# A fused attention and two-layer kernel on one core: new order of the first three attention groups, identity products on TensorE, and a new order of the exponential in the middle stage

## The chip, the cores and the metric

The kernel runs on one core of a Trainium2 chip. A core has TensorE (PE; its weight loads are shown apart, as PEld), VectorE (DVE), ScalarE (ACT), GpSimd (POOL) and SyncE (SP), which here issues nearly all DMAs. Each engine takes its instructions in the order in which the program issues them to it. The metric is the time of one execution in microseconds (us) on the device.

## The reference

Chunked attention (batch 4, 8 heads, 768 tokens, 64 wide; chunks of 32 queries look at 16 keys before the chunk, the chunk, 8 keys after it, and 8 memory keys) is followed by two dense blocks over 3072 tokens:

```python
x = attention(q, k, v, mem_k, mem_v)          # 3072 x 512
h = x @ w_in                                  # 512 -> 2048
x = where(h > 0, h, exp(min(h, 0)) - 1) @ w_out   # 2048 -> 512
out = ((x @ w1) * (x @ w2)) @ w3 @ w_out2     # 512 -> 1024 -> 1024 -> 512
```

All inputs and outputs are fp32.

## The kernel before

**Precision.** Each fp32 operand of the large products is split into a high part (a cast on ACT, `hi`) and a rest (a subtraction on DVE, `lo`), and each product becomes three (`mm3`, L124 to L126). The weights come raw from memory (512 KB a job); the `Feed` prepares a job in three `feed.step()` calls: `rebase` on ACT, `shift` and `low` on DVE a step later, then `hi_of` on ACT and `lo_of` on DVE (L172, L175) another step later. A step also issues the load of a job four to eight places on. There are 32 such jobs.

**Attention** works on 24 groups of 128 queries. A group passes through ten stages: `at_turn` (eight transposes on PE, three copies on ACT), `at_turn2`, `at_scores` (64 small products), `at_max` (DVE, then the exponential on ACT), `at_sum`, `at_norm`, `at_flip` (DVE), `at_values` (64 small products), `at_out` (hi on ACT, lo on DVE). `load_qk` and `load_v` issue its DMAs on SP in pieces of 256 bytes a row and head. Groups 1 and 2 have tiles of their own; group 3 and all later ones use the tiles of group 0.

**Start.** The first three groups fill the 384 tokens of block 0. The order of their stages and of the first five feed steps (`f`) is written out by hand in the string `START` (L69): `t u s m z n p v o` with a digit are the stages of that group. After it come the loads of group 3 (L607, L608). The feed's first five raw loads and all loads of groups 0 to 2 are issued ahead of it.

**Main loop.** Step n (0 to 129) belongs to block j = n // 16 and feature tile f = n % 16. It has `mm_h(n)` (12 matmuls into the PSUM bank `PS[4 + n % 2]`), `elu_exp(n)` (two ACT operations that read that bank), `elu_max(n)` (DVE, last reader of the bank, so `mm_h(n + 2)` waits for it), `elu_hi` (ACT), `elu_lo` (DVE), and `mm_x(n - 2)` (12 matmuls). In the first two steps of a block `mm_x(n - 2)` comes ahead of `mm_h(n)`, elsewhere behind it. In step 16j + 1 `store_x1` copies the finished block out of PSUM: four copies, alternately on ACT and DVE, through the pool `f_p` of four buffers, which the jobs of the middle stage use too, and four DMAs to `x1d`. While n < 16 there are two feed steps in each step.

**Slots.** `at_step()` is called twice in a step and works off one slot each time. Group G's stages start at slot `base(G)` and lie at +0 (turn), +1 (turn2, load of the next group's q and k), +2 (scores), +3, +4, +5, +6 (flip), +8 (values, out), +9 (load of the next group's v). From group 6 on, each group brings one to three conversion jobs of later weights (rebase at +0, low at +1, split at +2, store to memory in the next slot; a second kind at +4, +5 and +9, with four transposes on PE, `mid_flip`).

After step 129 the weights of the second dense block are multiplied together, and the rest is dense products. The change touches none of that.

Of the kernel before, what the change touches and what calls it, by code (L numbers as in the profile page):

```python
# [19 lines left out]
def tile_kernel(  # L20
# [24 lines left out]
    P = 128  # L45
# [15 lines left out]
    GPB = TB // GQ  # L61
    FF1 = w_in.shape[1] // P
# [3 lines left out]

    LATER = (10, 11, 12, 13, 14, 15, 25, 26, 27, 28, 29, 30, 31)

    START = "t0 u0 f s0 t1 f m0 u1 s1 z0 n0 m1 p0 t2 v0 u2 s2 f z1 n1 p1 o0 m2 v1 f z2 n2 p2 o1 v2 f o2"  # L69
    SCALE = 1.0 / float(D) ** 0.5  # L70
    assert GQ == P and KEYS == 64 and KT == 4 and HP == 4 and DM == 512

# [8 lines left out]
    ident = const.tile([P, P], F32, name="ident")  # L81
# [168 lines left out]
    def load_qk(G):  # L250
        if G >= NG:
            return
        b, g = divmod(G, GPS)
        t0 = g * GQ - LEFT
        p0, n1 = max(0, -t0), min(LEFT + RIGHT, S - t0 - P)
        kn_g = k_t[G] = at_tile(G, qk_p, [P, 2, H, D], "kn") if 0 < G < GPB else kn
        q_t[G] = at_tile(G, qk_p, [GQ, H, D], "qn")
        eng = nc.scalar if G == 0 else nc.sync
        eng.dma_start(out=q_t[G], in_=by_token(q, b, g * GQ, (g + 1) * GQ))
        nc.sync.dma_start(out=kn_g[p0:P, 0], in_=by_token(k, b, t0 + p0, t0 + P))  # L260
        nc.sync.dma_start(out=kn_g[0:n1, 1], in_=by_token(k, b, t0 + P, t0 + P + n1))
        if g == 0 or G < GPB:
            nc.sync.dma_start(out=kn_g[LEFT + RIGHT:CH, 1], in_=by_token(mem_k, b, 0, NM))

    def load_v(G):
        if G >= NG:
            return
        b, g = divmod(G, GPS)
        t0 = g * GQ - LEFT
        p0 = max(0, -t0)  # L270
        vw_g = v_t[G] = at_tile(G, v_p, [P, 2, H, D], "vw") if 0 < G < GPB else vw
        nc.sync.dma_start(out=vw_g[p0:P, 0], in_=by_token(v, b, t0 + p0, t0 + P))
        for c in range(NCG):
            t1 = t0 + (c + 1) * CH
            n1 = min(LEFT + RIGHT, S - t1)
            nc.sync.dma_start(out=vw_g[c * CH:c * CH + n1, 1], in_=by_token(v, b, t1, t1 + n1))
            if g == 0 or G < GPB:
                nc.sync.dma_start(out=vw_g[c * CH + LEFT + RIGHT:(c + 1) * CH, 1], in_=by_token(mem_v, b, 0, NM))
# [147 lines left out]
        slots.setdefault(int(at), []).append((at, len(slots.get(int(at), ())), fn, arg))  # L426

    def base(G):
        return 2 * FF1 * (G - GPB) // GPB, "slow"

    GM = 2 * GPB
    others = [Job((raw_rows, w_out2, c, 0), store=wod[c]) for c in range(FF2)]
# [21 lines left out]
    def at_step():  # L454
        store_next()
        for _, _, fn, arg in sorted(slots.pop(slot_at[0], ()), key=lambda x: x[:2]):
            fn(arg)
        slot_at[0] += 1
# [19 lines left out]
    def elu_max(n):  # L478
        e = eg_t[n]
        nc.vector.scalar_tensor_tensor(out=e, in0=e, scalar=-1.0, in1=h_t.pop(n), op0=ALU.add, op1=ALU.max)  # L480
# [5 lines left out]
    def elu_lo(n):  # L486
        g = g_t[n]
        nc.vector.tensor_tensor(out=g[:, 1, :], in0=eg_t.pop(n), in1=g[:, 0, :].bitcast(F32), op=ALU.subtract)  # L488
# [82 lines left out]
    with tc.manual_schedule():  # L571
        def weight(i):
            if i < FF1:
                return Job((raw_cols, w_in, i), slot=i)
            return Job((raw_rows, w_out, i - FF1, 0), slot=i)

        jobs, due = [], {}
        order = sorted(range(2 * FF1), key=lambda i: i if i < FF1 else i - FF1 + 2)
        for i in order:
            due[i] = len(jobs)  # L580
            jobs.append(weight(i))
        first_late = min(due[i] for i in LATER)
        feed = Feed(jobs)

        load_qk(0)
        make_identity(nc, ident)
        nc.gpsimd.memset(kn[0:LEFT, 0], 0.0)
        nc.gpsimd.memset(vw[0:LEFT, 0], 0.0)
        for c in range(NCG):
            for s in range(2):  # L590
                nc.gpsimd.memset(odd[c * CH:(c + 1) * CH, s], float(c % 2 == s))
        feed.load(1)
        load_qk(1)
        feed.load(2)
        load_v(0)
        load_qk(2)
        load_v(1)
        feed.load(3)
        load_v(2)
        feed.load(5)  # L600
        one = dict(t=at_turn, u=at_turn2, s=at_scores, m=at_max, z=at_sum, n=at_norm, p=at_flip, v=at_values, o=at_out)
        for what in START.split():
            if what == "f":
                feed.step()
            else:
                one[what[0]](int(what[1]))
        load_qk(GPB)  # L607
        load_v(GPB)  # L608
        early_psum.close()
        psum_x = ctx.enter_context(tc.tile_pool(name="psum_x", bufs=1, space=PSUM))  # L610
        for i in range(KT):
            PS[i] = psum_x.tile([P, 512], F32, name=f"bank{i}")
        NH = NB * FF1
        for n in range(NH + 2):
            j, f, at, last = seq[n] if n < NH else (NB, n - NH, n - NH, False)
            first = at < 2 and n >= 2
            if j == NB - 1 and f == 0:
                store_next()
                mid_ctx.close()
                at_ctx.close()  # L620
                late = ctx.enter_context(tc.tile_pool(name="late", bufs=1, side="right"))
                ab_jobs = [(c, r) for c in range(FF2) for r in range(2)]
            if n == FF1:
                feed.until(len(feed.jobs) - 1)
                raw_ctx.close()
                mid_ctx = ExitStack()
                pools["raw"] = mid_ctx.enter_context(tc.tile_pool(name="raw2", bufs=2, side="right"))
                pools["st"] = mid_ctx.enter_context(tc.tile_pool(name="st_p", bufs=2, side="right"))
                mid_load(2)

            def x():
                if n >= 2:
                    if n < FF1 + 2:
                        feed.until(due[FF1 + seq[n - 2][1]])
                    mm_x(n - 2)
                    if at == 1 and n < NH:
                        store_x1(j - 1)
                if n < FF1:
                    feed.step()
                at_step()  # L640

            if first:
                x()
            if n < NH:
                if j == 0:
                    feed.until(due[f])
                mm_h(n)
            if 1 <= n <= NH:
                elu_hi(n - 1)
            if n < FF1:  # L650
                feed.step()
            if 1 <= n <= NH:
                elu_lo(n - 1)
            at_step()
            if n < NH:
                elu_exp(n)
            if not first:
                x()
            if n < NH:
                elu_max(n)  # L660
            if n >= NH - FF1:

                free = [f] if n < NH else []
                if n >= NH - FF1 + 2:
                    free.append(FF1 + n - 2 - (NH - FF1))
                for slot in free:
                    if len(s_wo) < FF2 and len(s_wo) <= len(s_w3):
                        fill(slot, wod[len(s_wo)])
                        s_wo.append(slot)
                    elif len(s_w3) < 2 * FF2:  # L670
                        half, c = divmod(len(s_w3), FF2)
                        fill(slot, w3d[half][c])
                        s_w3[half, c] = slot
                    else:
                        c, r = ab_jobs.pop(0)
                        fill(slot, wabd[c][r])
                        s_ab[c, r] = slot
            if j == NB - 1:
                if f == 4:
                    load_x1(0)  # L680
                if f == 8:
                    split_x1(0)
                    load_x1(1)
        store_x1(NB - 1)
        for half in range(2):
            for c in range(FF2):
                for i in range(KT):
                    mm_wc(half, c, i)
                    if c == FF2 - 1:
                        keep_wc(half, i)  # L690
            for i in range(KT, FF2):
                c, r = ab_jobs.pop(0)
                fill(s_w3[half, i], wabd[c][r])
                s_ab[c, r] = s_w3[half, i]
        NA = NB * FF2
        for n in range(NA + 1):
            j, f = divmod(n, FF2)
            if n < NA:
                mm_ab(n)
                if f == 2 and j + 1 < NB:  # L700
                    split_x1(j + 1)
                    if j + 2 < NB:
                        load_x1(j + 2)
            if n >= 1:
                mm_o(n - 1)
                if f == 0:
                    store_out(j - 1)
# [30 lines left out]
```

## Time and profile before

| | |
|---|---|
| median of 3 runs | 1154.38 us (1153.18 to 1154.81) |
| the profiled execution | 1155.27 us |
| its span, first to last instruction | 1153.3 us |
| mean granted TensorE clock | 0.986 of full speed |
| PE busy / weight loads | 1096.8 us (95%) / 1029.9 us (89%) |
| DVE busy | 493.8 us (43%) |
| ACT busy | 431.1 us (37%) |
| chain that ended last, by engine | PE 81%, DVE 8%, ACT 5%, DMA 3% |

The shares are averages over stages with different limits: the first 55 us hold the first groups, 55 to 138 us the steps that prepare the weights, 138 to 660 us the middle, and what follows is dense. So a change is read from the stage in which it acts, and there from the wait that ends last. Times in rows count from the start of the span.

### The profile page before, as it was taken

What the parts mean: (1) busy time and instruction counts of PE and PEld (TensorE: products, weight loads), DVE (VectorE), ACT (ScalarE), POOL (GpSimd) and SP (SyncE); (2) the same over time, 40 slices, a digit from 0 to 9 for tenths busy, and PEclk for the clock granted to TensorE, in tenths of its full rate; (3) what the DMA queues carried; (4) which work ended last, traced back from release to release, by engine and by line L of the source; (5) the groups of instructions that cost most, each with busy time, mean ns of one, the idle gap of its engine ahead of it and who ended that gap; (6) DMA issues with size and microseconds to landing.
All of it is one profiled execution on the core that took longest, in us unless ns stands there. A gap on an engine that the chain in (4) does not pass through costs nothing.

```text
span 1153.3 us, 20889 instructions
## 1 busy us (share of the span) xinstructions
PE 1096.8 (95%) x8800; PEld 1029.9 (89%) x8800; DVE 493.8 (43%) x912; ACT 431.1 (37%) x897; POOL 2.1 (0%) x16
## 2 busy tenths in 40 slices
PE   4688999999999999899999999999999999999998
PEld 3588889989989899899899998799999999999997
DVE  4699655565565465555555331121222212222121
ACT  3477544454454444445444341121221212222111
POOL 0000000000000000000000000000000000000000
PEclk8699999999999999999999999999999999999999
DMA  8957344543633543544531785310000101000000
GB/s 171 288 143 205 99 150 120 158 135 109 175 110 110 173 128 109 157 129 128 155 105 40 251 286 178 109 45 28 28 28 28 55 1 56 28 28 28 1 28 28
DMA packets 153100, 124.78 MB, mean 108 GB/s; under 512 B 103856, under 2 KB 136624, under 8 KB 153008
## 3 DMA queue, kind: packets, MB, share of 16 engines
q1 hardware_dynamic: 151968, 123.20, 36.3%
q8 instruction: 69, 1.13, 0.4%
q10 hardware_dynamic: 1040, 0.26, 0.1%
q14 instruction: 23, 0.19, 0.1%
HBM read 89.88 MB, written 33.55 MB: 107 GB/s over the span
## 4 chain that ended last, share of the span: by engine, by line
PE 81%; DVE 8%; ACT 5%; DMA 3%; issue 2%; SPq 0%; DVEq 0%; ACTq 0%
PE bank L124 21%; PE bank L125 20%; PE bank L126 20%; PE banks L124 4%; PE banks L126 4%; PE banks L125 4%; DMA x1d<-st 2%; PE banks L376 2%; DVE w L175 1%; DVE g L488 1%; DVE eg L480 1%; PE banks L317 1%; DVE e L354 1%; ACT w L172 1%; PE banks L291 1%
## 5 line engine op out<-in xcount | busy, mean ns | idle before, releaser
L124 PE MATMUL bank<-xhl,w 128*128 128x384 f32 x768 | 266.4, 347 | 17.5 <-DVE eg L480 16.8
L126 PE MATMUL bank<-xhl,w 128*128 128x384 f32 x768 | 259.3, 338 | 0.0
L125 PE MATMUL bank<-xhl,w 128*128 128x384 f32 x768 | 259.2, 338 | 0.0
L124 PE MATMUL bank<-g,w 128*128 128x384 f32 x512 | 176.0, 344 | 0.0
L125 PE MATMUL bank<-g,w 128*128 128x384 f32 x512 | 172.5, 337 | 1.7 <-DVE g L488 0.8
L126 PE MATMUL bank<-g,w 128*128 128x384 f32 x512 | 171.5, 335 | 0.0
L124 PEld LDWEIGHTS bank<-xhl,w 128*128 128x128 f32 x768 | 145.6, 190 | 27.5 <-DVE eg L480 21.6
L552 DVE TENSOR_TENSOR eg<-eg,banks 128x384 f32<-128x384 f32 x64 | 35.5, 554 | 271.7 <-PE banks L126 271.7
L125 PEld LDWEIGHTS bank<-xhl,w 128*128 128x128 f32 x768 | 145.7, 190 | 3.2 <-DVE xhl L121 0.4
L126 PEld LDWEIGHTS bank<-xhl,w 128*128 128x128 f32 x768 | 145.4, 189 | 0.0
L488 DVE TENSOR_TENSOR g<-eg,g 128x384 fp32r<-128x384 f32 x128 | 71.3, 557 | 108.2 <-ACT g L484 108.2
L484 ACT CAST g<-eg 128x384 fp32r<-128x384 f32 x128 | 65.7, 513 | 127.0 <-DVE eg L480 127.0
L125 PEld LDWEIGHTS bank<-g,w 128*128 128x128 f32 x512 | 96.2, 188 | 4.8 <-DVE g L488 4.7
L124 PEld LDWEIGHTS bank<-g,w 128*128 128x128 f32 x512 | 96.1, 188 | 2.2
L126 PEld LDWEIGHTS bank<-g,w 128*128 128x128 f32 x512 | 96.1, 188 | 0.0
L551 ACT COPY eg<-bank 128x384 f32<-128x384 f32 x64 | 30.7, 480 | 170.4 <-PE bank L126 170.4
L480 DVE SCALAR_TENSOR_TENSOR eg<-eg,bank 128x384 f32<-128x384 f32 x128 | 69.9, 546 | 56.0 <-ACT eg L475 55.7
L120 ACT CAST g<-eg 128x384 fp32r<-128x384 f32 x64 | 32.8, 512 | 141.4 <-DVE eg L552 141.4
L124 PE MATMUL banks<-xhl,w 128*128 128x384 f32 x256 | 85.5, 334 | 0.0
L125 PE MATMUL banks<-xhl,w 128*128 128x384 f32 x256 | 85.5, 334 | 0.0
L126 PE MATMUL banks<-xhl,w 128*128 128x384 f32 x256 | 85.5, 334 | 0.0
L474 ACT ACTIVATE eg<-bank 128x384 f32<-128x384 f32 x128 | 62.8, 490 | 48.4 <-PE bank L126 47.8
(101 smaller groups left out, 1404.9 us busy)
## 6 DMA issues: line engine op xcount, KB each, us to landing
raw<-in_moe_w_dram SPq DMA_DIRECT2D x32, 512.0 KB
raw<-in_moe_w_out_dram SPq DMA_DIRECT2D x20, 512.0 KB
w3d<-st SPq DMA_DIRECT2D x16, 512.0 KB
wabd<-st SPq DMA_DIRECT2D x16, 512.0 KB
w<-w3d SPq DMA_DIRECT2D x16, 512.0 KB
w<-wabd SPq DMA_DIRECT2D x16, 512.0 KB
raw<-in_moe_w_in_dram SPq DMA_DIRECT2D x12, 512.0 KB
x1d<-st SPq DMA_DIRECT2D x32, 192.0 KB
```

The lines of the kernel that those rows point to most:

```text
L120: nc.scalar.copy(hi, src)
L124: mm(o, lhsT=w_hi, rhs=x_hi, start=start, stop=False)
L125: mm(o, lhsT=w_hi, rhs=x_lo, start=False, stop=False)
L126: mm(o, lhsT=w_lo, rhs=x_hi, start=False, stop=stop)
L172: nc.scalar.copy(job.to[:, 0, :], job.f if src is None else src)
L376: mm(o, lhsT=vw[cc, u, 2 * hp + r, :], rhs=pT[cc, r, hp, u, :], start=u == 0, stop=u == 1)
L474: nc.scalar.activation(e, h_t[n], AF.Relu, scale=-1.0)
L480: nc.vector.scalar_tensor_tensor(out=e, in0=e, scalar=-1.0, in1=h_t.pop(n), op0=ALU.add, op1=ALU.max)
L484: nc.scalar.copy(g_t[n][:, 0, :], eg_t[n])
L488: nc.vector.tensor_tensor(out=g[:, 1, :], in0=eg_t.pop(n), in1=g[:, 0, :].bitcast(F32), op=ALU.subtract)
L551: nc.scalar.copy(e, pab[0])
L552: nc.vector.tensor_tensor(out=e, in0=e, in1=pab[1], op=ALU.mult)
```

## The change

Three things are edited. `START` gets a new order: feed steps three to five move behind stages of groups 1 and 2, the loads of group 3 (`k3`, `w3`) move from behind the string into it, and `d` with a digit issues that many products of the 128 x 128 identity with itself (34 in all) into a PSUM bank that nobody reads. `base(G)` is one slot later. In the main loop from step 16 on, `elu_exp(n)` is issued ahead of the slot that follows `mm_h(n)`, and `elu_hi(n)`, `elu_lo(n)` follow `elu_max(n)` in the same step.

```diff
-    START = "t0 u0 f s0 t1 f m0 u1 s1 z0 n0 m1 p0 t2 v0 u2 s2 f z1 n1 p1 o0 m2 v1 f z2 n2 p2 o1 v2 f o2"
+    START = "d9 t0 d3 u0 f s0 t1 d3 f m0 u1 s1 d3 z0 n0 m1 p0 t2 v0 u2 d1 s2 d7 z1 n1 p1 m2 o0 k3 w3 v1 d8 z2 n2 p2 f o1 v2 f o2 f"
...
     def base(G):
-        return 2 * FF1 * (G - GPB) // GPB, "slow"
+        return 2 * FF1 * (G - GPB) // GPB + 1, "slow"
...
+        def keep_busy(n):
+
+            for _ in range(n):
+                mm(PS[5][:, 0:P], lhsT=ident, rhs=ident, start=True, stop=True)
+
-        one = dict(t=at_turn, u=at_turn2, s=at_scores, m=at_max, z=at_sum, n=at_norm, p=at_flip, v=at_values, o=at_out)
+        one = dict(t=at_turn, u=at_turn2, s=at_scores, m=at_max, z=at_sum, n=at_norm, p=at_flip, v=at_values, o=at_out, k=load_qk, w=load_v, d=keep_busy)
...
-        load_qk(GPB)
-        load_v(GPB)
...
-            if 1 <= n <= NH:
+            spread = n < FF1
+            if 1 <= n <= FF1:
                 elu_hi(n - 1)
-            if n < FF1:
+            if spread:
                 feed.step()
-            if 1 <= n <= NH:
+            if 1 <= n <= FF1:
                 elu_lo(n - 1)
+            if n < NH and not spread:
+                elu_exp(n)
             at_step()
-            if n < NH:
+            if spread:
                 elu_exp(n)
             if not first:
                 x()
             if n < NH:
                 elu_max(n)
+            if n < NH and not spread:
+                elu_hi(n)
+                elu_lo(n)
```

## Rows read from the trace of the kernel before

**Rows 1.** Busy us and count by engine in stretches; clock, DMA share, GB/s.
```profile
core 0: us, PE busy (x) PEld busy (x) DVE busy (x) ACT busy (x) POOL busy (x), PEclk, DMA share, GB/s
...
60.00:110.00 50.00, 42.17 (x418) 39.63 (x417) 47.23 (x90) 35.69 (x73) 0.00 (x0) 1.00 0.60 168
150.00:660.00 510.00, 495.45 (x4907) 471.29 (x4906) 277.77 (x515) 244.78 (x515) 0.00 (x0) 1.00 0.45 132
```

**Rows 2.** PE's waits, 150 to 660 us: total us, times, longest us.
```profile
PE bank L124 <- DVE eg L480: 13.0, 12, 1.4
```

**Rows 3.** Instructions in order of time around group 3's turn: PE, ACT, DVE.
```profile
46.50 1.10 PE L291 MATMUL banks<-ident,kn 128*128 128x128 f32 x4 [0.66 <-DMA kn<-in_k_dram]
...
47.64 0.58 ACT L293 COPY qT<-banks 128x512 f32<-128x512 f32 x1 [7.31 <-PE banks L291]
...
42.00 0.69 DVE L167 SCALAR_TENSOR_TENSOR f<-more,f 128x512 int32<-128x512 int32 x1
50.51 0.69 DVE L175 TENSOR_TENSOR w<-f,w 128x512 fp32r<-128x512 f32 x1 [7.82 <-ACT w L172]
...
52.77 0.69 DVE L175 TENSOR_TENSOR w<-f,w 128x512 fp32r<-128x512 f32 x1
```

**Rows 4.** SP's DMA issues, in order of time.
```profile
30.63 0.37 SPq L140 DMA_DIRECT2D raw<-in_moe_w_in_dram  x1
31.11 0.75 SPq L148 DMA_DIRECT2D raw<-in_moe_w_out_dram  x1
...
38.04 0.33 SPq L148 DMA_DIRECT2D raw<-in_moe_w_out_dram  x1
38.46 0.39 SPq L259 DMA_DIRECT2D qn<-in_q_dram  x1
```

**Rows 5.** Stretches as in rows 1: raw weights moving, then group 3's rows.
```profile
35.00:41.50 6.50, 4.39 (x70) 3.80 (x71) 5.70 (x10) 1.68 (x3) 0.00 (x0) 0.50 1.07 389
42.50:46.50 4.00, 1.78 (x9) 1.22 (x7) 0.19 (x1) 0.00 (x0) 0.00 (x0) 0.92 1.19 209
```

**Rows 6.** DVE's other idle times in the start, and a norm.
```profile
24.06 0.69 DVE L175 TENSOR_TENSOR w<-f,w 128x512 fp32r<-128x512 f32 x1 [2.00 <-ACT w L172]
...
26.03 1.29 DVE L354 TENSOR_TENSOR e<-e,rc 128x512 f32<-128x512 f32 x2
...
39.28 0.69 DVE L121 TENSOR_TENSOR xhl<-pair,xhl 128x512 fp32r<-128x512 f32 x1 [0.70 <-ACT xhl L120]
```

**Rows 7.** PE's small products at different times of the start.
```profile
5.67 1.09 PE L289 MATMUL banks<-ident,qn 128*128 128x128 f32 x4 [5.67 <-DMA qn<-in_q_dram]
...
36.40 2.22 PE L376 MATMUL pair<-pT,vw 64*64 64x64 f32 x64 [5.51 <-DVE pT L365]
```

**Rows 8.** Group 5's flip on DVE, and mm_h(16) on PE.
```profile
126.81 1.24 DVE L365 STREAM_TRANSPOSE pT<-e 128x1024 f32<-128x1024 f32 x1
...
138.01 0.42 PE L124 MATMUL bank<-xhl,w 128*128 128x384 f32 x1
```

**Rows 9.** PE's work where nothing waits: mm_h, mm_x, values, transposes, scores.
```profile
58.70 0.33 PE L124 MATMUL bank<-xhl,w 128*128 128x384 f32 x1
...
60.78 0.33 PE L124 MATMUL bank<-g,w 128*128 128x384 f32 x1
...
185.36 1.16 PE L376 MATMUL banks<-pT,vw 64*64 64x64 f32 x64
...
193.28 0.60 PE L289 MATMUL banks<-ident,qn 128*128 128x128 f32 x4
...
199.00 0.86 PE L317 MATMUL banks<-kT,qT 64*32 64x64 f32 x64
```

**Rows 10.** The first block boundary: mm_x(15), mm_h(21); SP's stores; DVE.
```profile
140.67 0.45 PE L124 MATMUL bank<-g,w 128*128 128x384 f32 x1
...
163.99 0.42 PE L124 MATMUL bank<-xhl,w 128*128 128x384 f32 x1
...
142.35 0.35 SPq L148 DMA_DIRECT2D raw<-in_moe_w_out_dram  x1
142.79 5.08 SPq L501 DMA_DIRECT2D x1d<-st  x4
...
146.97 0.56 DVE L117 COPY st<-bank 128x384 f32<-128x384 f32 x1 [3.76 <-DMA x1d<-st]
...
151.84 0.56 DVE L480 SCALAR_TENSOR_TENSOR eg<-eg,bank 128x384 f32<-128x384 f32 x1 [1.69 <-ACT eg L475]
```

**Rows 11.** DVE's waits for the stores, 142 to 660 us: total, times, longest.
```profile
DVE st L117 <- DMA x1d<-st: 23.1, 6, 4.4
```

## The prediction

> **What bounds the kernel now.** The busy shares say TensorE (95% of the span), so I first split the span by stage. Between 60 and 110 us DVE is busy 47.2 of 50 us and PE 42.2; between 150 and 660 us PE is busy 495 of 510 us and DVE little over half [rows 1]. So the stage that prepares the weights is set by DVE, and whatever lets DVE start that work earlier moves everything behind it; the middle is set by PE, and only PE's waits can be won there. From 660 us on PE is dense and the change doesn't reach it.
>
> In the middle, PE's waits add up to 13.0 us in 12 times, all of them `mm_h` waiting for `elu_max` [rows 2]. Twelve times in six block boundaries is twice a boundary: 1.4 us, then 13.0 / 6 - 1.4 = 0.8 us. The reader should see in the boundary's rows where DVE lost the time: the fourth copy of `store_x1` starts at 146.97, after 3.76 us of idling for the DMA of the first copy, because the pool has four buffers and a job holds one [rows 10]; this happens at six boundaries, 23.1 us in all [rows 11].
>
> In the start, the largest hole is group 3's turn. It stands first in step 0, PE waits for its k rows until 46.50, ACT sits idle behind it for 7.31 us up to 47.64, and DVE, whose next `lo` needs ACT's `hi`, for 7.82 us up to 50.51 [rows 3]. The cause is on SP: the loads of group 3 go out at 38.46, behind three raw loads, of 31.11 to 38.04, the last of which waited for the fourth feed step to free its buffer [rows 4].
>
> **Loads of group 3.** In the new `START` `k3` and `w3` stand ahead of the third feed step, so behind the raw load of 30.63 and ahead of the three that follow [rows 4]. Their buffers (group 0's) are free by then. Three jobs of 512 KB, 1.57 MB, no longer precede them; raw loads move at 389 GB/s [rows 5], so that is 4.0 us, and the k rows land at 46.50 - 4.0 = 42.5. At best they land so early that DVE never waits for them; at worst the DMA engines deliver them as now, at 46.50.
>
> What is put behind pays: the three raw loads, which belong to feed steps 9 to 11, wait for group 3's q, k and v rows, about 1 MB at 209 GB/s [rows 5], 5 us. They land near 47 to 50; step 9 comes near 48 by the walk below. That cover is thin (1 to 3 us), and a microsecond beyond it is a microsecond of DVE. Group 4's q and k go out one slot later, ten slots ahead of need: nothing.
>
> **Order of `START` and the first steps.** I walk DVE's queue with its own spacings. Up to the second `low` of the next feed job after `elu_max(0)` the same instructions are issued in both versions, ending at 52.77 before. Of the idle times, 7.82 us is the loads', 2.00 us at 24.06 (the third feed step's `lo` behind a `hi` that waits for group 2's turn2) and 0.70 us at 39.28 [rows 3, 6] go, since the feed steps now come after flips; a new one of about 1.3 us appears where `o0` waits for the exponential of `m2` on ACT. DVE alone could be at this point 7.8 + 2.0 + 0.7 - 1.3 = 9.2 us earlier, at 43.6. The next `lo`, however, needs ACT, which does group 3's copies first. From k's landing to that `lo` it was 52.77 - 46.50 = 6.3 us; in the new order `elu_exp(0)` and one feed step (1.0 + 1.2 us and their hand-overs, 3.2 us in all) are ahead of the turn, one slot later, and no longer inside. So: 42.5 + 3.1 = 45.6, a gain of **7.2 us**. Bounds: 9.2 (DVE alone), and 52.77 - 46.50 - 3.1 = 3.2 (loads as now).
>
> At the other end of this stage group 5's flip ends at 128.05, and `mm_h(16)` starts at 138.01 [rows 8]; in between lie values, `mm_h(15)`, two `mm_x` and group 6's turn. One slot later, flip and values of group 5 come after `mm_h(15)`'s operand is ready, so `mm_h(15)` runs beside the flip. DVE then has 1.7 us more ahead of the flip (an `elu_max`, two `lo`), the PE sequence behind it is 1.2 + 2 x 2.1 us [rows 9] instead of 9.9, and the turn (twice 0.60 less its overlap, 0.8 us) comes later: 9.9 - 5.4 - 1.7 - 0.8 = **2 us**. Start together: 9.2, between 5 and 11.
>
> **Identity products.** There is no full fp32 product of this shape in the trace. The nearest rows are four transposes in 0.60 to 1.09 us [rows 7, 9], so 0.15 to 0.27 us each; as a product might cost double, I keep 0.54 as the upper end: 34 of them are 5 to 18 us of PE. They stand where PE idles: nine ahead of the first q rows (idle to 5.67 [rows 7]; 1.4 to 4.9 us), groups of one or three while ACT copies, seven and eight ahead of `at_values` of groups 1 and 2, which wait for flips, 5.51 us for the last one [rows 7]. I cost them at nothing, with 2 us if covers fail, which the late k rows would still hide.
>
> Their gain is the clock. At 36.40 the values product took 2.22 us, with 0.50 granted (the 1.2 GHz level); at full clock it takes 1.16 [rows 5, 7, 9]. The first transposes, too, took 1.09 against 0.60 us. But behind them the start waits for the k rows, so a faster PE ends in a longer wait: nothing, up to the 9.2 us bound.
>
> **The exponential's place and the boundary.** Outside the boundaries the queues on ACT and DVE hold the same work in the same cyclic order (`max`, `hi`, `lo`), with the exponential ahead of a slot's ACT work instead of behind; PE doesn't wait there now [rows 2], so nothing is to be had. At a boundary, from `mm_x(15)` to `mm_h(21)` it takes 163.99 - 140.67 = 23.3 us [rows 10]. The work is eight runs of twelve matmuls at 2.08 us, scores 0.86, values 1.16 and a `mid_flip` like four transposes, 0.60 [rows 9]: 19.3. So 4.0 us are lost: 2.2 in `mm_h` [rows 2], the rest in `mm_x` waiting for a late `lo` and in restarts.
>
> Now, the fourth copy: ACT reaches the first copy about 1.3 us later (copies of the turn, `rebase` and `hi(16)` precede it), but the raw load of 142.35 that goes out just ahead of the stores [rows 10] moves behind them with the slot, 512 KB or 1.3 us less: the DMA wait ends at the same place. After that copy, DVE took 4.9 us up to the end of `elu_max(17)`: the job's `lo`, `lo(16)`, group 6's max, and 1.69 us waiting for the exponential, which ACT did behind the group's own [rows 10]. In the new order `lo(16)` is done before, the max a slot later, and the exponential early; `shift` and `low` (1.1) and a hand-over to ACT (0.6) come in: 2.9 us. So the wait of 1.4 goes, and those in `mm_x` (0.8) as well. The second one, 0.8, stays, as max, exponential and sum of the group now lie between `elu_max(17)` and `elu_max(18)`, and the values of this group will wait some 0.4 for the flip behind. Lost: about 2 instead of 4. Six times 2.0 is **12 us**. Bounds: if the store's DMA takes as long as now the copy is 1.3 later, 0.9 a boundary, 5 us; if DVE keeps up everywhere, 2.9, 17 us.
>
> **Sum.** 9.2 + 12 = 21.2 us less: 1155.3 - 21.2 = 1134.1 for the profiled execution, which is 0.9 above the median of the runs: 1133.
>
> **Rivals.** *Start only*: the second wait and the values' wait grow by what the first one loses, since DVE has one queue of work behind the late copy; the 3.76 us that speak for it remain. 1154.4 - 9.2 = 1145. *Middle only*: group 3's rows land as before, or the raw loads put behind starve the feed, so the start gives its lower 3 us; 1154.4 - 12 - 3 = 1139. Against it: SP's order is a fact of the program. *Clock*: with the added products the transposes run in 0.60 instead of 1.09 us and the values in 1.16 instead of 2.22 from the first group on [rows 7, 9], the start's chain moves ahead by 2 us, and early k rows let DVE use its whole 9.2 us (11 with the flip); with the boundary's upper end, 1154.4 - 11 - 17 = 1126. Against it: the start waits for k rows, not for PE [rows 3]. The Trainium skill ("TensorE: Matmul & The Clock Gate", Part 4, PE-mode transpose) says that transposes don't count as activity for the clock as products do; by that rule the added products are what raises it in this rival, and without them it would stay as in the rows. *Slower*: `lo(n)` right behind `max(n)` makes DVE wait for ACT's cast (0.6 us); a group's norm 1.29, `shift` and `low` 1.1 and flip 1.24 with `max` and `lo` [rows 3, 6, 8, 10] make 4.7 us of DVE in one step, against 4.2 us of PE. If each of the 18 groups of the middle then stops PE for the 1.4 us that a boundary costs now, with no boundary better, it is +25 - 9 = +16: 1170. It decides from 0.5 us a group on. Against it: DVE is busy 54% there and the same cycle runs now without a wait. *No change*: both gains absent, 1154.
>
> **How the numbers follow.** Forecast (both, 1126 to 1141) 0.62, start only 0.13, middle only 0.12, clock 0.04, no change 0.04, slower 0.05. Faster by over 0.2% (2.3 us, about what a measurement can tell): 0.62 + 0.13 + 0.12 + 0.04 = 0.91. The range runs from 1126, the upper bounds of both gains together, to 1146, which takes in the start alone.
>
> **What would show it.** Right: k of group 3 ends PE's wait near 42.5; DVE's idle time around 40 to 51 us falls from 7.8 to 2 to 3; `mm_h(16)` starts near 129; of the twelve waits for `elu_max` in the middle about six are left, near 0.8 us; DVE's wait for the stores remains. Wrong: raw loads ending DVE's or ACT's waits near 48 to 52; identity products running when q rows or flips have long been ready; new PE waits at groups away from boundaries.

## The result and the profile after

The changed kernel took 1128.42 us (median of 4, 1127.33 to 1128.94) against 1154.6 before: a ratio of 0.9774, 95% interval 0.9757 to 0.9791, so 26 us less where 21 were forecast. The profiled execution took 1127.33 us, its span is 1125.3: 28.0 us less than the profiled one of before, and that is the difference that the traces can account for.

I split the 28.0 us at two places on PE: the start of `mm_h(16)`, where the stage that prepares the weights ends, and the stretch from `mm_x(15)` to `mm_x(111)`, which holds six block boundaries and the attention of blocks 1 to 6. `mm_h(16)` moved from 138.01 [rows 8] to 129.88 and `mm_x(15)` from 140.67 [rows 10] to 132.75, 7.9 us; the stretch behind it shrank from 495.8 to 475.8 us, 20.0. Behind that nothing changed: the sum is 27.9. But the profiled execution of before had a late start. Three of the kernels below change nothing ahead of step 16, and their `mm_h(16)` starts at 136.1, 136.1 and 137.7. By the medians, 26.2 - 20.0 leaves 6.2 us for the start and not 7.9.

**The middle.** PE's waits between 135 and 640 us in the changed kernel (total us, times, longest); this is the whole list:

```profile
PE banks L289 <- DVE st L175: 0.2, 1, 0.2
```

All twelve waits of [rows 2] are gone. The stretches of [rows 1] now read (same columns):

```profile
core 0: us, PE busy (x) PEld busy (x) DVE busy (x) ACT busy (x) POOL busy (x), PEclk, DMA share, GB/s
...
60.00:110.00 50.00, 43.26 (x472) 40.30 (x471) 45.71 (x84) 35.44 (x74) 0.00 (x0) 0.97 0.62 177
150.00:600.00 450.00, 449.64 (x4619) 430.50 (x4618) 260.27 (x483) 224.82 (x478) 0.00 (x0) 1.00 0.47 135
```

PE is busy 449.6 of 450 us in the middle, with DVE still at 58%. The waits were 13.0 us, the stretch became 20.0 shorter. PE's busy time in it (same columns), before and changed:

```profile
140.67:636.50 495.83, 481.04 (x4877) 455.95 (x4877) 275.61 (x511) 237.63 (x502) 0.00 (x0) 1.00 0.44 128
```

```profile
132.75:608.57 475.82, 475.46 (x4883) 455.37 (x4882) 274.64 (x510) 237.38 (x505) 0.00 (x0) 1.00 0.47 135
```

So 14.4 us of the 20.0 are idle time of PE (14.8 before, 0.4 changed), and 5.6 us are the same work taking less busy time. What shortens it isn't isolated here. The first boundary in the changed kernel, as in [rows 10]: PE, then SP, then DVE:

```profile
132.75 0.42 PE L124 MATMUL bank<-g,w 128*128 128x384 f32 x1
...
152.29 0.44 PE L124 MATMUL bank<-xhl,w 128*128 128x384 f32 x1
...
135.82 2.90 SPq L501 DMA_DIRECT2D x1d<-st  x4
138.81 1.77 SPq L259 DMA_DIRECT2D qn<-in_q_dram  x1
...
142.16 0.34 SPq L148 DMA_DIRECT2D raw<-in_moe_w_out_dram  x1
...
137.82 0.56 DVE L117 COPY st<-bank 128x384 f32<-128x384 f32 x1 [1.34 <-PE bank L126]
...
140.73 0.54 DVE L480 SCALAR_TENSOR_TENSOR eg<-eg,bank 128x384 f32<-128x384 f32 x1
...
145.70 0.55 DVE L480 SCALAR_TENSOR_TENSOR eg<-eg,bank 128x384 f32<-128x384 f32 x1
```

The stores now go out ahead of the q, k and raw loads, and the fourth copy starts 137.82 - 135.82 = 2.0 us after the first store's issue; it was 4.2 [rows 10]. (The profile names PE as the releaser, but the matmuls that wrote this bank were done by 135.1. The copy waits for several semaphores; the one of the first store had the last of its updates in this trace at 137.70, so it is the store that it waited for.) `elu_max(17)` ends at 141.3, 1.5 us ahead of `mm_h(19)`, and `elu_max(18)` at 146.3, 0.7 ahead of `mm_h(20)`. From `mm_x(15)` to `mm_h(21)` it is 19.5 us instead of 23.3. DVE's waits ahead of that copy, 135 to 640 us, are 8.8 us in two rows, against 23.1 us in [rows 11]. All six waits are for the store, which lands 0.1 us ahead of the copy at every boundary:

```profile
DVE st L117 <- PE bank L126: 6.8, 5, 1.4
...
DVE st L117 <- DMA x1d<-st: 2.0, 1, 2.0
```

**The start.** Group 3's turn, as in [rows 3], and SP, as in [rows 4]:

```profile
40.92 1.12 PE L291 MATMUL banks<-ident,kn 128*128 128x128 f32 x4 [0.18 <-DMA kn<-in_k_dram]
...
42.07 0.58 ACT L293 COPY qT<-banks 128x512 f32<-128x512 f32 x1 [0.88 <-PE banks L291]
...
40.64 0.69 DVE L175 TENSOR_TENSOR w<-f,w 128x512 fp32r<-128x512 f32 x1 [1.17 <-ACT w L172]
...
44.41 0.69 DVE L175 TENSOR_TENSOR w<-f,w 128x512 fp32r<-128x512 f32 x1 [1.55 <-ACT w L172]
...
29.21 0.37 SPq L140 DMA_DIRECT2D raw<-in_moe_w_in_dram  x1
29.68 0.47 SPq L259 DMA_DIRECT2D qn<-in_q_dram  x1
...
40.06 0.36 SPq L148 DMA_DIRECT2D raw<-in_moe_w_out_dram  x1
```

The k rows are there at 40.9 instead of 46.5, ACT's hole of 7.3 us is 0.9, DVE's hole of 7.8 is 1.2 and 1.6, and the `lo` that stood at 52.77 stands at 44.41: 8.4 us earlier. But of these 8.4 only part arrives at the end of the stage. Group 5's flip and `mm_h(16)`, as in [rows 8]:

```profile
123.11 1.24 DVE L365 STREAM_TRANSPOSE pT<-e 128x1024 f32<-128x1024 f32 x1
...
129.88 0.33 PE L124 MATMUL bank<-xhl,w 128*128 128x384 f32 x1
```

The flip is only 3.7 us earlier. Of the 4.7 us between, 1.7 are the work that its later slot puts ahead of it. Most of the rest is in DVE's waits from behind that `lo` up to the flip (before from 53 to 127 us, changed from 45.2 to 123.1 us):

```profile
DVE w L175 <- ACT w L172: 3.3, 6, 1.1
```

```profile
DVE w L175 <- ACT w L172: 5.5, 7, 1.1
DVE xhl L121 <- ACT xhl L120: 0.5, 2, 0.3
```

That is 6.0 us against 3.3. Waits of over 1 us for a feed step's `hi` now come four times, before twice; in three of the four a group's exponential or its turn copies stand ahead of that `hi` on ACT. PE then makes up for it, as `mm_h(15)` (120.98) runs ahead of group 5's values instead of behind them (129.98 before): from the flip's end to `mm_h(16)` it is 5.5 us instead of 10.0.

### The profile page after: what moved, and what is told of

Same layout as the page of the kernel before. It is cut to its first block, busy times and chain, and to the rows that moved or that the text cites. A ratio compares the mean times of both kernels' runs of the same rounds, so it can differ in the third digit from the quotient of the medians.

```text
span 1125.3 us, 21004 instructions
## 1 busy us (share of the span) xinstructions
PE 1099.0 (98%) x8868; PEld 1036.9 (92%) x8868; DVE 493.6 (44%) x912; ACT 430.2 (38%) x897; POOL 2.1 (0%) x16
## 4 chain that ended last, share of the span: by engine, by line
PE 87%; DVE 4%; ACT 4%; DMA 3%; SPq 1%; issue 1%; ACTq 0%; DVEq 0%
PE bank L124 23%; PE bank L126 22%; PE bank L125 22%; PE banks L124 4%; PE banks L125 4%; PE banks L126 4%; PE banks L376 2%; DMA vw<-in_v_dram 1%; PE banks L317 1%; DMA kn<-in_k_dram 1%; ACT w L172 1%; DVE w L175 1%; ACT g L484 1%; PE banks L289 1%; PE banks L291 1%
## 5 line engine op out<-in xcount | busy, mean ns | idle before, releaser
L484 ACT CAST g<-eg 128x384 fp32r<-128x384 f32 x128 | 65.7, 514 | 161.5 <-DVE eg L480 161.5
```

The source lines that it names most:

```text
L484: nc.scalar.copy(g_t[n][:, 0, :], eg_t[n])
```

## The experiments

A row's ratio compares it with executions of the kernel before that were taken beside it (medians from 1153.2 to 1154.6 us). "mm_h(16)" is its start in the trace, "middle" the stretch from `mm_x(15)` to `mm_x(111)`. A single execution's start varies: the first raw load behind the v rows went out on SP anywhere from 25.4 to 27.7 us in these traces (27.7 in the one of before), so a difference in `mm_h(16)` under 2 us proves little; the middle repeats within 0.8 us where nothing in it was edited.

| kernel | median us | ratio to before, 95% interval | mm_h(16) | middle |
|---|---|---|---|---|
| before | 1154.6 | | 138.0 | 495.8 |
| changed | 1128.4 | 0.9774 (0.9757 to 0.9791) | 129.9 | 475.8 |
| changed, no products | 1127.4 | 0.9774 (0.9759 to 0.9790) | 129.4 | 475.5 |
| changed, group 3's loads behind | 1131.8 | 0.9814 (0.9798 to 0.9830) | 133.0 | 476.2 |
| changed, slots as before | 1131.7 | 0.9821 (0.9798 to 0.9843) | 129.6 | 480.6 |
| changed, loop as before | 1130.0 | 0.9799 (0.9781 to 0.9816) | 128.6 | 478.9 |
| before, new loop | 1138.6 | 0.9873 (0.9859 to 0.9888) | 136.1 | 480.4 |
| before, slots later | 1134.3 | 0.9836 (0.9820 to 0.9852) | 133.8 | 478.7 |
| before, stores first | 1139.4 | 0.9876 (0.9861 to 0.9891) | 137.6 | 481.1 |
| changed, old feed order, no products | 1130.8 | 0.9803 (0.9789 to 0.9818) | 133.8 | 475.7 |
| before, exponential moved | 1142.0 | 0.9907 (0.9890 to 0.9924) | 137.7 | 485.1 |
| before, hi and lo moved | 1152.7 | 0.9993 (0.9981 to 1.0006) | 136.1 | 496.6 |
| no products, later slots from group 6 | 1128.3 | 0.9791 (0.9777 to 0.9806) | 130.9 | 475.6 |
| no products, later slots from group 5 | 1127.2 | 0.9787 (0.9772 to 0.9801) | 129.9 | 475.4 |

### What the start is made of

**Without the identity products.**

```diff
-    START = "d9 t0 d3 u0 f s0 t1 d3 f m0 u1 s1 d3 z0 n0 m1 p0 t2 v0 u2 d1 s2 d7 z1 n1 p1 m2 o0 k3 w3 v1 d8 z2 n2 p2 f o1 v2 f o2 f"
+    START = "t0 u0 f s0 t1 f m0 u1 s1 z0 n0 m1 p0 t2 v0 u2 s2 z1 n1 p1 m2 o0 k3 w3 v1 z2 n2 p2 f o1 v2 f o2 f"
```

> The changed kernel without its 34 identity products, nothing else. Theory (the start waits for group 3's k rows and for DVE, not for PE): the clock is lower in the start, but mm_h(16) moves by less than 1 us (129 to 131) and the time stays within 1.5 us of 1128.4. Rival (the products' clock brings part of the start's gain): groups 0 to 2 end 2 to 3 us later, so do group 3's turn and mm_h(16) (132 to 133), and the time is 1131 to 1133.

1127.4 us and `mm_h(16)` at 129.4, as the theory said: the products bring nothing. In the changed kernel, PE's products on the identity:

```profile
1.36 4.21 PE L604 MATMUL bank<-ident 128*128 128x128 f32 x18 [1.36 <-POOL ident masks.py:199]
...
27.49 2.05 PE L604 MATMUL bank<-ident 128*128 128x128 f32 x16
```

The trace has two records for each product: nine took 4.2 us at first (0.47 each), eight took 2.05 at full clock (0.26 each), inside my bounds of 0.15 to 0.54. They did change the clock (from 25 to 30 us 0.87 of full speed was granted, without them 0.50), and group 0's flip ended at 18.6 instead of 20.7 us. But `mm_h(0)` and the turn still found it at the 1.2 GHz level, as this stretch of the changed kernel shows (columns as in [rows 1]):

```profile
35.00:40.00 5.00, 4.27 (x13) 3.76 (x14) 4.36 (x9) 2.21 (x5) 0.00 (x0) 0.50 1.06 235
```

Without the products the next stretch, with group 3's turn, even ran at full clock:

```profile
40.00:45.00 5.00, 3.42 (x24) 2.86 (x22) 3.53 (x7) 4.97 (x12) 0.00 (x0) 1.00 0.89 265
```

There `mm_h(0)` starts 1.4 us later (34.71 instead of 33.35), and the turn comes right behind it and waits for no DMA:

```profile
39.75 0.60 PE L289 MATMUL banks<-ident,qn 128*128 128x128 f32 x4
...
40.24 0.66 PE L291 MATMUL banks<-ident,kn 128*128 128x128 f32 x4
```

With the products PE is earlier and waits for the k rows until 40.92. So the `lo` that follows stands at 44.30 without them and at 44.41 with them. The Trainium skill says that a transpose doesn't count as activity for the clock as a product does ("TensorE: Matmul & The Clock Gate", Part 4, PE-mode transpose). These two kernels don't test that: the added products also filled time in which PE had been idle. What they sped up wasn't last.

**Group 3's loads behind the hand-written order** (`k3 w3` at its end; nothing else).

```diff
-... m2 o0 k3 w3 v1 d8 z2 n2 p2 f o1 v2 f o2 f"
+... m2 o0 v1 d8 z2 n2 p2 f o1 v2 f o2 f k3 w3"
```

> The changed kernel with the loads of group 3 behind the hand-written order again. Theory (their place on SP is most of the start's gain): k of group 3 lands 4 us later (about 45), mm_h(16) starts 3 to 4 us later (133 to 134), time 1131 to 1133. Rival (the later feed steps make the gain, and the loads are hidden by the slot that was added): mm_h(16) within 1 us of 129.9, time 1128 to 1129.5.

The theory's numbers: k's transposes 3.3 us later, `mm_h(16)` 3.1 us later, 1131.8 us. PE's k transposes and the DVE `lo` that follows:

```profile
44.23 1.12 PE L291 MATMUL banks<-ident,kn 128*128 128x128 f32 x4
...
47.72 0.69 DVE L175 TENSOR_TENSOR w<-f,w 128x512 fp32r<-128x512 f32 x1 [4.84 <-ACT w L172]
```

**The feed steps where they were, the loads early.**

```diff
-    START = "d9 t0 d3 u0 f s0 t1 d3 f m0 ... f o1 v2 f o2 f"
+    START = "t0 u0 f s0 t1 f m0 u1 s1 z0 n0 m1 p0 t2 v0 u2 s2 k3 w3 f z1 n1 p1 o0 m2 v1 f z2 n2 p2 o1 v2 f o2"
```

> The changed kernel with START as before, without identity products, and only the loads of group 3 moved, to just ahead of the third feed step. Theory (besides the loads, the later feed steps save DVE about 2.7 us of waiting for hi): mm_h(16) at 131 to 133 instead of 129.4 to 129.9, time 1129 to 1131. Rival (all of the start's gain is the loads): within 0.7 us of 129.9, 1127 to 1128.5.

1130.8, with `mm_h(16)` at 133.8, a little beyond the theory's range: the early loads alone bring nothing over the kernel before with later slots, which has it at 133.8 too. The k transposes of this kernel, and of that one:

```profile
44.51 0.60 PE L291 MATMUL banks<-ident,kn 128*128 128x128 f32 x4
...
48.63 0.69 DVE L175 TENSOR_TENSOR w<-f,w 128x512 fp32r<-128x512 f32 x1 [0.55 <-ACT w L172]
```

```profile
45.63 0.66 PE L291 MATMUL banks<-ident,kn 128*128 128x128 f32 x4 [0.44 <-DMA kn<-in_k_dram]
...
48.66 0.69 DVE L175 TENSOR_TENSOR w<-f,w 128x512 fp32r<-128x512 f32 x1 [0.62 <-ACT w L172]
```

With early loads and the old order the turn waits for no DMA; it comes right behind `mm_h(0)`, which starts at 39.94 as group 2's output is ready only then. With late loads the order hardly matters, as k lands at 44 to 46. So the start is the later of two: the end of `mm_h(0)`, whose start the feed order moved from 39.9 to 33.4, and the landing of k; the `lo` follows 3 to 4 us behind the k transposes in all of these. Each part alone leaves the other standing. The ratios agree: to the kernel before with later slots, both single parts differ by what the middle explains to within 1 us, and the changed kernel is 4 us better than that.

### What the middle is made of

**The slots put back.**

```diff
-        return 2 * FF1 * (G - GPB) // GPB + 1, "slow"
+        return 2 * FF1 * (G - GPB) // GPB, "slow"
```

> The changed kernel with the groups' slots as before (no + 1). Theory (the slot lets the stores of a block go out ahead of the job's raw load and the next group's loads, so the buffer comes free in 2 us, not 4): DVE's wait for the stores is back near 3.8 us at each of six boundaries, PE's waits at the boundaries are partly back, a boundary loses 1 to 2 us of the 3.3 gained, and the start loses 1 to 3 us because group 3's turn stands ahead of elu_exp(0): 1136 to 1142. Rival (the exponential's place alone makes the boundaries free of waits): only the start's part, 1129 to 1132.

1131.7 us, in the rival's range but not for its reason: DVE's wait for the stores is back, as the theory said (first two rows below, 135 to 640 us; the one wait put down to ACT ends as the store lands), but only 4.8 us of the middle's 20.0 go with it, 3.4 us as PE's waits (third row), and the start loses nothing.

```profile
DVE st L117 <- DMA x1d<-st: 14.1, 5, 3.6
DVE st L117 <- ACT eg L475: 3.6, 1, 3.6
...
PE bank L124 <- DVE eg L480: 3.4, 5, 0.9
```

**The loop's order put back** (the last hunk of the change undone).

> The changed kernel with the main loop's order as before (exponential behind the slot, hi and lo a step later). Theory (both the slot and the exponential's place are needed): the stores' wait stays short, but elu_max of the boundary's second step waits for the exponential behind the group's own ACT work, 0.7 to 1.5 us of PE wait a boundary come back: 1132 to 1138. Rival (the slot alone makes the middle's gain): 1128 to 1130.

1130.0 us, the middle 3.1 us longer: less than the theory's smallest number, and the rival's largest. With either slot or loop put back, most of the middle's gain stays. So I took them one at a time from the kernel before.

**The loop's order alone; the slot alone.**

```diff
+            spread = n < FF1
...
+            if n < NH and not spread:
+                elu_exp(n)
             at_step()
...
+            if n < NH and not spread:
+                elu_hi(n)
+                elu_lo(n)
```

> The kernel before with the new order of the main loop alone. The middle (from mm_x(15) to mm_x(111)) took 495.8 us before and 475.8 changed; with the slots put back it took 480.6. Theory (loop order and slot each remove most of the boundary's waits, their effects overlap): 15 us less in the middle, nothing in the start: 1138 to 1141. Rival (the loop's order pays only where the start has freed DVE and the DMA queue before the first boundary): under 8 us, 1146 or more.

```diff
-        return 2 * FF1 * (G - GPB) // GPB, "slow"
+        return 2 * FF1 * (G - GPB) // GPB + 1, "slow"
```

> The kernel before with every group's slots one later, nothing else. Theory (the slot alone lets the stores pass the raw load and moves the group's exponential off the boundary step): 14 to 18 us less in the middle, and the start within 2 us: 1135 to 1142. Rival (as for the loop's order alone): under 8 us, 1146 or more.

15.4 and 17.2 us less in the middle: both theories held (1138.6; 1134.3, just below its range). With the slot alone `mm_h(16)` stands 4.3 us earlier than in the trace of before, but that one was late: by the medians (1153.5 beside it, 1134.3) the slot gives the start 2.0 us. The two gains overlap, as either removes most of the same twelve waits: 3.6 us in 5 times are left with the loop's order alone, none with the slot alone.

**Only the order on SP**: slots and loop as before, but a job's raw load and the next group's q and k one slot later, so that the stores pass them.

```diff
-        "slow": (0, 1, 1, 2, 3, 4, 5, 6, 8, 8, 9), "fast": ...
+        "slow": (0, 1, 2, 2, 3, 4, 5, 6, 8, 8, 9), "fast": ...
...
         low(job)
-        mid_load(mid_jobs.index(job) + 3)
+
+    def mid_next(job):
+        mid_load(mid_jobs.index(job) + 3)
...
+                put(s0 + at + 2, mid_next, job)
...
+                    put(s0 + 5, mid_next, job)
```

> The kernel before with the slots and the loop as they were, but each job's raw load and the next group's q and k loads issued one slot later, so that at a boundary the stores of the finished block go out ahead of them. Theory (the late store is the cause of the boundary's loss, and its place on SP is what the slot changes): DVE's wait for the stores falls from 23.1 to under 12 us, the first PE wait of a boundary shrinks by what the copy is earlier: 6 to 12 us less, 1142 to 1148. Rival (the place of the group's DVE and ACT work in the boundary steps is what counts): DVE's wait falls, PE's waits for elu_max stay above 10 us, time within 3 us of 1154.

14.7 us less in the middle, 1139.4: the theory, with more than its size. DVE's wait for the stores fell from 23.1 to 7.3 us. SP and DVE at the first boundary (this kernel's `elu_max` is L484), and PE's wait from 135 to 650 us, against 13.0 us in 12 times:

```profile
142.06 2.90 SPq L505 DMA_DIRECT2D x1d<-st  x4
145.06 0.39 SPq L259 DMA_DIRECT2D qn<-in_q_dram  x1
...
144.06 0.56 DVE L117 COPY st<-bank 128x384 f32<-128x384 f32 x1 [1.29 <-ACT g L488]
...
148.94 0.56 DVE L484 SCALAR_TENSOR_TENSOR eg<-eg,bank 128x384 f32<-128x384 f32 x1 [1.70 <-ACT eg L479]
...
PE bank L124 <- DVE eg L484: 2.3, 6, 0.7
```

The copy starts 2.0 us after the stores' issue here too, and that alone takes most of the waits away, although DVE still waits 1.70 us for the exponential.

**The two halves of the loop's order, each alone.**

```diff
+            if n < NH and n >= FF1:
+                elu_exp(n)
             at_step()
-            if n < NH:
+            if n < FF1:
                 elu_exp(n)
```

> The kernel before with only the exponential moved ahead of the slot from step 16 on; hi and lo stay in the next step. Theory (the first wait of a boundary is elu_max waiting for an exponential that ACT does behind the group's own): nearly all of what the loop's order alone brought (15.4 us in the middle): 480 to 483 us from mm_x(15) to mm_x(111), 1138 to 1141. Rival (hi and lo a step earlier, so that mm_x never waits, make most of it): 488 us or more, 1146 or more.

```diff
-            if 1 <= n <= NH:
+            if 1 <= n <= FF1:
                 elu_hi(n - 1)
...
+            if n < NH and not spread:
+                elu_hi(n)
+                elu_lo(n)
```

> The kernel before with only elu_hi and elu_lo moved into the step of their elu_max from step 16 on; the exponential stays behind the slot. Theory: only mm_x's waits at the boundaries go, 0.4 to 0.7 us at each of six: 2 to 5 us, 1149 to 1152. Rival: most of the loop's gain, 1141 or less.

The exponential's place alone: 10.7 us in the middle, between theory and rival, nearer the theory. `hi` and `lo` alone: no change (0.9993, 0.9981 to 1.0006), the middle 0.8 longer; neither number was right. The two together give 15.4, so `hi` and `lo` bring 4.7 only once the exponential is early. What they do then I didn't isolate.

### Trying for more

The changed kernel without the products, its later slots kept from groups 3 to 5 or 3 and 4 only:

```diff
-        return 2 * FF1 * (G - GPB) // GPB + 1, "slow"
+        return 2 * FF1 * (G - GPB) // GPB + (G >= GM), "slow"
```

> The changed kernel without identity products and with the added slot only from group 6 on; groups 3 to 5 as before. Theory (the added slot costs DVE about 3 us of waiting for hi in the stage that prepares the weights, and gives back as much by running mm_h(15) beside the flip): group 5's flip ends near 121 instead of 124, mm_h(16) at 128.5 to 129.5, the middle as in the changed kernel: 1126 to 1128. Rival (group 3's turn ahead of elu_exp(0) costs, as k lands after it): mm_h(16) 131 or later, 1129 or more.

```diff
+        return 2 * FF1 * (G - GPB) // GPB + (G >= GM - 1), "slow"
```

> As late_slots, with the added slot from group 5 on. Theory: both of the effects named there, DVE's shorter waits for groups 3 and 4 and mm_h(15) beside group 5's flip: mm_h(16) at 127 to 129, 1125 to 1127.5. Rival: group 5's flip moves back by what its later slot puts ahead of it on DVE (1.7 us), and nothing is left: mm_h(16) 129 to 130, 1126.5 to 1128.5.

1128.3 and 1127.2: within their intervals neither differs from the changed kernel. The first lies between theory and rival; the second's `mm_h(16)` is the rival's. In both traces the `lo` behind group 3's turn came at 47.2 to 47.9 instead of 44.4, so the earlier slots seem to lose here what they save later; that isn't shown, as the first raw load behind the v rows also went out 0.8 and 2.0 us later in these two traces. No version that I ran is clearly faster than the changed one.

## Why the prediction held, and where it didn't

- *The stages and their bounds* held: PE set the middle, DVE with ACT the stage ahead of it; the whole gain was found in the two places named, none of it behind 660 us.
- *The loads of group 3*: forecast to land at 42.5, landed at 40.9; the `lo` moved by 8.4 us where 7.2 were forecast. Up to 1.5 us of the 8.4 are the late start of the trace of before (the same `lo` stands at 51.3, 51.3 and 52.7 in the three kernels that change nothing ahead of step 16). Against the kernel with the loads put behind again, the k transposes moved by 3.3 us where 4.0 were forecast. The mechanism was right. But the prediction added loads and feed order as one sum limited by k; the experiments show two arms of which the later counts, so neither alone is worth what the sum suggests (0 for the loads under the old order, 0.7 us for the order under late loads, 4 for both, on top of the later slot's 2 by the medians).
- *The end of the stage*: "2 us" for `mm_h(15)` beside the flip came out as a loss of 0.2 (8.4 us at the `lo`, 8.1 at `mm_h(16)`). The reordering happened, and the PE sequence shrank to 5.5 us where 5.4 were forecast; the step that failed is the silent one that a gain at the `lo` travels unchanged through 80 us of DVE-bound work. DVE waits 2.7 us more for ACT there (6.0 against 3.3), and that is the later slots' doing: with the slots put back it is 3.0 us.
- *The identity products at nothing*: held, shown by the kernel without them.
- *The boundary*, 12 us forecast, 20.0 measured, above its upper bound of 17: the mis-sized term. The step was "the DMA wait ends at the same place". I took 1.3 us off the store's 4.2 for the raw load ahead of it; it fell to 2.0, as the q and k loads moved behind the stores too, and the copy came 1.2 us sooner behind `mm_x(15)` (5.1 us instead of 6.3). From the copy to the end of `elu_max(17)` it took the 2.9 us forecast. That was early enough for the second wait (0.8) and the wait for the values, which I had left standing, to go as well: 3.3 us a boundary. DVE's wait for the stores, which was to remain, fell from 23.1 to 8.8 us.
- *Rivals*: none came. That `lo` right behind `max` would choke DVE is out: PE has a single wait of 0.2 us left in the middle. Nor does ACT or DVE wait for a raw load that was put behind.

The forecast time was right to 5 us, by a start 1.3 us too large in the traces (3.0 by the medians) and a middle 8 us too small. That it stayed in the range is partly luck: its lower end, 1126, is 28.4 us below 1154.4, and the middle's 20.0 with the start's forecast 9.2 would have been 29.2.

## What to carry to other kernels

When an engine waits for a buffer that a store must free, look at what was issued on the same queue just ahead of the store: here moving loads that nobody needed yet behind it gave 14.7 us in the middle with no other edit. When two things end at the same point (a load and the work ahead of it), price their maximum: each alone may show nothing. And 34 products that kept an idle TensorE busy paid nothing here, where TensorE didn't end last. Compare medians as well as traces: one late start in the trace of before made a 2 us gain look like 4.3.

## What the runs showed of the hardware

A plain fp32 product leaves two matmul records, a transpose of the same shape one, so a count of records isn't a count of products. The clock column of the changed kernel reads 1.00 in the first 5 us, while nine products from 1.36 on took 0.47 us each, as seven did at 23.19, where it reads 0.50; eight at 27.49, where it reads 1.00, took 0.26. So ahead of its first change, here at 5.79, the column isn't a measurement. In the kernel before it reads 1.00 up to 15 us in the same way, while four transposes took 1.09 us ([rows 7]). And with 34 products to keep PE busy the clock was still at the 1.2 GHz level when `mm_h(0)` came.
